# Shorter partition sums, three more low halves on VectorE, an uneven last tile and a new order

## The chip, the cores and the metric

The kernel runs on one core of one Trainium2 chip. A core has a matrix engine (TensorE, PE in the profile; its weight loads are shown as PEld), three engines for elementwise work (VectorE or DVE, ScalarE or ACT, GpSimd or POOL) and SyncE (SP), on whose queue this kernel issues its DMAs. Each engine works through its own stream of instructions in the order in which the kernel recorded them, and waits on semaphores for the others. The metric is the device time in microseconds of one execution, as a median of several.

## The reference

One token mixer with a gate, on x of 2048 tokens by 512 features. With LN for a layer norm without parameters:

```python
xn = LN(x)
# A: attention of 32 heads of 16 features; each token looks at itself and at 7 tokens before it, 2 apart
q, k, v = split(xn @ wqkv)
s = softmax(q . k[t - 0, 2, .., 14] / 4) @ v[t - 0, 2, .., 14] @ wo
# B: an MLP of 1376 hidden features
h = gelu(LN(xn) @ w1 + b1)
g = silu(h @ w2 + b2)
out = x + s * g
```

Tokens that lie before the first are masked in A.

## The kernel before

The host lays x out in two halves (even and odd tokens, `c` = 0 and 1), so that the steps of 2 become steps of 1; each half has 8 tiles of 128 tokens. Numbers in fp32 are fed to TensorE as two fp16 parts: a high part (the rounded number times a power of two) and a low part (the rest); a product is three matmuls, high by high, high by low and low by high. To choose the powers of two, the kernel sums the squares of every weight tensor: ScalarE sums along each partition, and a matmul against a matrix `fours` (128 x 128, every element 4.0) adds over the partitions and gives the sum to all of them (`total`, the matmuls on lines 488 and 493). VectorE then takes the exponent of that sum and makes scales from it.

The work has these parts, by line of the profile:

- Layer norm of the 16 tiles and transposes to features by tokens (`ln0`, lines 690 to 735, for half 0; `ln1`, lines 749 to 765, for half 1).
- 8 attention units (half `c` by group `hb` of 8 heads). TensorE makes q, k and v of a unit (`qkv`, L795 and L802; 96 matmuls of 384 columns for most units); ScalarE, or VectorE for a few, evicts them from PSUM into one of two tiles `U` (L817, L813); DMAs copy shifted rows of k and v (the halo, L825 to L831); VectorE does the attention with products and sums over 2048 numbers per partition (`attention`, L865 and L869 for the logits, L900 to L908 for the softmax, L934, L976 and L929 for the values), helped by GpSimd (L958). The result is split into parts (`emit_o`, L917 and L919) and transposed by DMA (L922) into `oT`.
- The MLP in 44 steps: 4 chunks of 512 tokens by 11 blocks of 128 hidden features. Step p is 12 matmuls into a PSUM tile `mh` (`mlp1`, L1090), GELU on ScalarE (L1107), the high half on ScalarE (L1111) and the low half. The low half has two ways. For the steps in `DVE_LO` VectorE makes it in one instruction (L1115). For the others TensorE subtracts the high half within PSUM, by a matmul against a diagonal matrix `dg` (L1121), and ScalarE reads the rest (L1124). Two steps later 12 matmuls of `mlp2` (L1137) add the block into four PSUM tiles `z`, which ScalarE turns into the gate by SiLU (L1153; L1148 for the last chunk).
- The output projection, 12 matmuls a tile (L1004): for half 0 between the MLP steps, on the two PSUM tiles `ps` that `qkv` uses too (`wo_first`, evicted by VectorE at L1018, added at L995 or on GpSimd at L997); for half 1 at the end (`wo_last`). There the first 9 matmuls of each tile run ahead of the last attention unit's result, the last 3 behind it; VectorE multiplies with the gate (L1069), x is added (L995, L997) and a DMA stores the tile (L998). The last tile is done in two parts of 256 columns, with lines 1060, 1063 and 1065 in place of these.
- `WAKE0 + WAKE` = 34 matmuls of 256 columns against `fours`, read as bf16, whose result nobody uses (L1239): they fill TensorE in the start.

None of this is written in the order of execution. Each operation is given to a planner (`Plan.add`) with an engine, a length, what it reads and writes, and a priority; `issue` orders them all with a list scheduler and records them. With `judge` and `draw` the lengths are varied by a chain of random seeds (`SEEDS`); the chain decides which order comes out. The planner's lengths set the order only.

Of the kernel before, what the change touches and what calls it, by code (L numbers as in the profile page):

```python
# [9 lines left out]
F32 = mybir.dt.float32  # L10
F16 = mybir.dt.float16
BF16 = mybir.dt.bfloat16
# [7 lines left out]
P = 128  # L20
S, D, F = 2048, 512, 1376
# [5 lines left out]
NHB = 4  # L27
# [31 lines left out]

BEFORE_W1 = (0, 1, 4, 5)  # L60

DVE_LO = (*range(4), *range(12, 44))


class Buf:
# [5 lines left out]
    @property  # L71
    def t(self):
        return self.ring.tiles[self.slot]
# [18 lines left out]
class Plan:  # L92
# [245 lines left out]

SEEDS = ((100197, 519502, 511555, 636945, 242082, 583485, 986620, 484517, 932055, 691004, 181636),)

# [45 lines left out]
def tile_mixer(ctx, tc, a_x, a_wqkv, a_wo, b_w1, b_b1, b_w2, out):  # L388
    nc = tc.nc
    pl = Plan()  # L390
# [9 lines left out]
    sb = ctx.enter_context(tc.tile_pool(name="sb", bufs=1))  # L400
# [15 lines left out]
    def dma(nbytes, fn, r, w, **k):  # L416
        pl.add("sp", 0.0, fn, r, w, nbytes=nbytes, **k)

    xv, ov = a_x, out

    PR_H, PR_U, PR_M = 200.0, 1000.0, 1000000.0

    ident = sb.tile([P, P], F32, name="ident")
    make_identity(nc, ident)
    fours = sb.tile([P, P], F32, name="fours")
    nc.vector.memset(fours, 4.0)
    halves = sb.tile([P, 16], F32, name="halves")
    nc.gpsimd.memset(halves[:, 0:8], -0.5)
    nc.gpsimd.memset(halves[:, 8:16], 0.5)
# [11 lines left out]
    oT = sb.tile([P, NHB, 2, 2, 4, P], F16, name="oT")  # L441
# [40 lines left out]

    def total(dst, dkey, cols, n, ckeys, late=False, apart=False):

        b = (R_ps if late else R_z[0]).new()
        if apart:
            for k in range(2):
                pl.add("pe", 0.15, lambda k=k: nc.tensor.matmul(
                    b.t[:, 0:1], fours, cols()[:, k:k + 1], start=(k == 0), stop=(k == 1)),
                    [ckeys[k]], [b], prio=min(pl.prio, PTOT))  # L490
            n = 1
        else:
            pl.add("pe", 0.15, lambda: nc.tensor.matmul(b.t[:, 0:n], fours, cols()[:, 0:n], start=True,
                                                       stop=True), ckeys, [b], prio=min(pl.prio, PTOT))
# [71 lines left out]
    def prep_q(hb):  # L566
# [426 lines left out]
    def finish(c, i, t, tkey, x, eng="dve"):  # L993
        if eng == "dve":
            dve(512, lambda: nc.vector.tensor_tensor(t(), t(), x(), op=ALU.add), tkey, tkey[:1])  # L995
        else:
            pool(1.2, lambda: nc.gpsimd.tensor_tensor(t(), t(), x(), op=ALU.add), tkey, tkey[:1])  # L997
        dma(P * 2048, lambda: nc.sync.dma_start(ov[c, i], t()), tkey[:1], [("out", c, i)], tail=0.7)  # L998

    def wo_mm(b, i, hbs, last=NHB - 1, cols=slice(0, D)):  # L1000
        def mm():
            for hb in hbs:
                for n, (s, t) in enumerate(((0, 0), (0, 1), (1, 0))):
                    nc.tensor.matmul(b.t[:, cols], oT[:, hb, i // 4, s, i % 4], wo[:, t, hb, cols],  # L1004
                                     start=(hb == 0 and n == 0), stop=(hb == last and n == 2))
        return mm
# [19 lines left out]
    def wo_last():  # L1026
        rings = [R_ps, R_ps, R_mh, R_mh] + R_z
        tiles = []

        halfs = [slice(h * 256, h * 256 + 256) for h in range(2)]  # L1030
        for i in range(NI):
            b = rings[i].new()
            bh = [b, rings[0].new()] if i == NI - 1 else [b]
            r = [("oT", hb, i // 4) for hb in range(NHB - 1)] + [("wo", k) for k in (0, 2)]
            if i < NI - 1:
                pe(9, 512, wo_mm(b, i, range(NHB - 1)), r, [b], prio=PR_M * 10 + 2 * i)
            else:

                for h in range(2):
                    pe(9, 256, wo_mm(bh[h], i, range(NHB - 1), cols=halfs[h]), r, [bh[h]], prio=PR_M * 10 + 2 * i + h)  # L1040
            tiles.append(bh)
        for i in range(4):
            dma(P * 2048, lambda i=i: nc.sync.dma_start(gu[i], gd[1, i]),
                [("gd", 1, i), ("U0end",)], [("gu", i)], prio=PR_M * 10)
        for i in range(NI):
            b = tiles[i][0]
            if i < 7:
                xb = R_f.new()
                x, xkey = (lambda xb=xb: xb.t), xb
            else:  # L1050
                x, xkey = (lambda: U[0][:, NI * D:(NI + 1) * D]), ("gux",)
            dma(P * 2048, lambda x=x, i=i: nc.sync.dma_start(x(), xv[1, i]),
                [("oT", NHB - 2, 0), ("U0end",)], [xkey], prio=PR_M * 10 + i)
            t = lambda i=i: gu[i]
            if i == NI - 1:
                for h in range(2):
# [3 lines left out]
                    dve(256, lambda b=b, t=t, cols=cols: nc.vector.scalar_tensor_tensor(  # L1060
                        t()[:, cols], b.t[:, cols], osc[:, 2:3], t()[:, cols], op0=ALU.mult, op1=ALU.mult),
                        [b, ("gu", i), ("osc",)], [("gu", i, h)], port=False, c=0.14)
                    dve(256, lambda t=t, x=x, cols=cols: nc.vector.tensor_tensor(  # L1063
                        t()[:, cols], t()[:, cols], x()[:, cols], op=ALU.add), [("gu", i, h), xkey], [("gu", i, h)])
                    dma(P * 1024, lambda i=i, t=t, cols=cols: nc.sync.dma_start(ov[1, i][:, cols], t()[:, cols]),
                        [("gu", i, h)], [("out", 1, i, h)], tail=0.7)
                continue
            pe(3, 512, wo_mm(b, i, [NHB - 1]), [("oT", NHB - 1, i // 4)], [b], prio=PR_M * 10 + 2 * i + 1)
            dve(512, lambda b=b, t=t: nc.vector.scalar_tensor_tensor(  # L1069
                t(), b.t, osc[:, 2:3], t(), op0=ALU.mult, op1=ALU.mult),  # L1070
                [b, ("gu", i), ("osc",)], [("gu", i)], port=False, c=0.14)
            finish(1, i, t, [("gu", i), xkey], x, "pool" if i % 2 == 0 else "dve")
# [8 lines left out]
    def mlp1(ch, f):  # L1081
# [24 lines left out]
        with prio(PR_H + pl.prio * 1e-6):  # L1106
# [6 lines left out]
                [b] + [("hseq", NF * ch + f - 1)] * (NF * ch + f > 0), [hk, ("hseq", NF * ch + f)])  # L1113
            if NF * ch + f in DVE_LO:
                dve(512, lambda: nc.vector.scalar_tensor_tensor(  # L1115
# [76 lines left out]
    def zero_halo(b):  # L1192
        pool(0.85, lambda: nc.gpsimd.memset(U[b][0:1, KH * P:(KH + 7) * P], 0.0), [],
             [("kz", b)])
# [38 lines left out]
        f()  # L1233
    zero_halo(0)
    zero_halo(1)
    idle = fours.bitcast(BF16)
    for n in range(WAKE0 + WAKE):
        b = R_z[0].new()
        pl.add("pe", 0.2 if n < 16 else 0.1, lambda b=b: nc.tensor.matmul(b.t[:, 0:2 * P], idle[:, 0:P], idle, start=True,  # L1239
                                                       stop=True), [("yd", 2)] if n >= WAKE0 else [], [b], prio=1e9)  # L1240
# [136 lines left out]
    for u, (c, hb) in enumerate(units):  # L1377
# [62 lines left out]
```

## Time and profile before

| | |
|---|---|
| median of 3 runs | 414.87 us (414.87 to 415.22) |
| the profiled execution | 414.88 us, of which the span of the profile is 413.0 |
| TensorE busy | 408.2 us (99%), 2112 matmuls |
| TensorE weight loads | 210.3 us (51%) |
| VectorE busy | 383.7 us (93%), 367 instructions |
| ScalarE busy | 224.2 us (54%) |
| GpSimd busy | 104.2 us (25%) |
| granted clock of TensorE | 1.00 |

A row of a group reads: line, engine, operation, what is written <- what is read, sizes, count | busy us, mean ns of one | idle time of the engine just before, and what ended it. A row of the timeline reads: start, length, engine, line, operation, count, and in brackets the idle time before it with its releaser. In the chain that ended last a row is start, length and what, and each piece starts where the one before it ended. Lengths of matmuls in groups and timelines include the time until the result is out, which lies beside the next matmul; the distance from start to start is what one costs in a stream.

### The profile page before, as it was taken

What the parts mean: (1) busy time and instruction counts of PE and PEld (TensorE: products, weight loads), DVE (VectorE), ACT (ScalarE), POOL (GpSimd) and SP (SyncE); (2) the same over time, 40 slices, a digit from 0 to 9 for tenths busy, and PEclk for the clock granted to TensorE, in tenths of its full rate; (3) what the DMA queues carried; (4) which work ended last, traced back from release to release, by engine and by line L of the source; (5) the groups of instructions that cost most, each with busy time, mean ns of one, the idle gap of its engine ahead of it and who ended that gap; (6) DMA issues with size and microseconds to landing.
All of it is one profiled execution on the core that took longest, in us unless ns stands there. A gap on an engine that the chain in (4) does not pass through costs nothing.

```text
span 413.0 us, 5592 instructions
## 1 busy us (share of the span) xinstructions
PE 408.2 (99%) x2112; PEld 210.3 (51%) x2112; DVE 383.7 (93%) x367; ACT 224.2 (54%) x362; POOL 104.2 (25%) x154
## 2 busy tenths in 40 slices
PE   8999999999999999999999999999999999999996
PEld 5666444445544554456444654445655554444443
DVE  5989999999899999999799979999989999999947
ACT  4999998979469477323663271126411492244500
POOL 7620531003900250015000510055036500250004
PEclk9999999999999999999999999999999999999999
DMA  7972360130253638300650061201053375008025
GB/s 282 414 278 78 110 210 0 63 116 1 71 123 126 143 95 173 61 2 0 150 194 1 2 135 57 102 0 56 22 179 114 102 203 166 2 0 241 16 51 203
DMA packets 42666, 44.83 MB, mean 109 GB/s; under 512 B 27496, under 2 KB 27936, under 8 KB 42128
## 3 DMA queue, kind: packets, MB, share of 16 engines
q1 hardware_dynamic: 42640, 44.49, 35.6%
q8 instruction: 16, 0.26, 0.3%
q14 instruction: 10, 0.08, 0.1%
HBM read 23.53 MB, written 7.34 MB: 75 GB/s over the span
## 4 chain that ended last, share of the span: by engine, by line
PE 97%; DVE 1%; DMA 1%; POOL 0%; issue 0%
PE z L1137 28%; PE ps L795 27%; PE mh L1090 26%; PE ps L1004 6%; PE mh L795 2%; PE z L1004 2%; PE mh L1004 1%; PE ps L1090 1%; PE z L697 1%; PE mh L802 1%; DMA prod<-in_A_x_dram 1%; PE ps L802 1%; PE mh L1121 0%; DVE U L1063 0%; PE z L1239 0%; DVE U L1060 0%
## 5 line engine op out<-in xcount | busy, mean ns | idle before, releaser
L1090 PE MATMUL mh<-yT,w 128*128 128x512 f16 (+1 forms) x504 | 115.5, 379 | 0.0
L795 PE MATMUL ps<-wq,yT 128*128 128x384 f16 x684 | 114.8, 326 | 0.0
L1137 PE MATMUL z<-w,h 128*128 128x512 f16 x480 | 110.7, 379 | 0.0
L795 PEld LDWEIGHTS <-yT 128*128 128x128 f16 x744 | 72.7, 98 | 48.2
L1090 PEld LDWEIGHTS <-w 128*128 128x128 f16 (+1 forms) x528 | 52.9, 100 | 60.8
L1107 ACT ACTIVATE mh<-mh,b1T,hsc 128x512 f32<-128x512 f32 (+1 forms) x42 | 31.4, 748 | 88.5 <-PE mh L1090 88.5
L1137 PEld LDWEIGHTS <-h 128*128 128x128 f16 x480 | 47.0, 98 | 55.6
L865 DVE TENSOR_TENSOR prod<-U 128x2048 f32<-128x2048 f32 x32 | 73.0, 2283 | 1.3 <-DMA U<-U 1.1
L869 DVE TENSOR_REDUCE L<-prod 128x128 f32<-128x2048 f32 x32 | 73.0, 2281 | 0.8
L817 ACT ACTIVATE U<-ps,cs 128x384 f32<-128x384 f32 x57 | 33.0, 579 | 59.9 <-PE ps L795 58.1
L934 DVE TENSOR_TENSOR prod<-L,U 128x2048 f32<-128x2048 f32 x28 | 63.3, 2286 | 0.2
L957 POOL COPY gate<-prod 1x1 f32<-1x1 f32 x21 | 3.6, 174 | 210.6 <-DVE prod L865 210.6
L929 DVE TENSOR_TENSOR prod<-prod,prod 128x2048 f32<-128x2048 f32 x16 | 36.5, 2284 | 0.0
L958 POOL TENSOR_TENSOR prod<-prod 128x1024 f32<-128x1024 f32 x14 | 32.9, 2347 | 0.0
L1004 PEld LDWEIGHTS <-oT 128*128 128x128 f16 x204 | 20.0, 98 | 21.5
L1004 PE MATMUL ps<-wo,oT 128*128 128x512 f16 (+1 forms) x132 | 28.8, 369 | 0.0
L1111 ACT ACTIVATE h<-mh,hsc 128x512 f16<-128x512 f32 x38 | 25.8, 683 | 0.7
L1115 DVE SCALAR_TENSOR_TENSOR h<-mh,hsc,h 128x512 f16<-128x512 f32 x31 | 22.9, 744 | 2.5 <-ACT h L1111 2.3
L958 POOL TENSOR_TENSOR prod<-prod,prod 128x1024 f32<-128x1024 f32 x7 | 16.4, 2346 | 0.0
L997 POOL TENSOR_TENSOR f<-f,f 128x512 f32<-128x512 f32 x4 | 10.6, 2640 | 22.6 <-DVE f L1018 20.6
L997 POOL TENSOR_TENSOR U<-U,f 128x512 f32<-128x512 f32 x4 | 5.9, 1469 | 34.5 <-DVE U L1069 34.5
L919 DVE SCALAR_TENSOR_TENSOR o<-prod,osc,o 128x1024 f16<-128x1024 f32 (+1 forms) x9 | 10.4, 1151 | 3.6 <-ACT o L917 3.6
(182 smaller groups left out, 395.0 us busy)
## 6 DMA issues: line engine op xcount, KB each, us to landing
f<-in_A_x_dram SPq DMA_DIRECT2D x31, 256.0 KB, 3.5
U<-U SPq DMA_DIRECT2D x16, 392.0 KB, 4.0
gd<-f SPq DMA_DIRECT2D x12, 256.0 KB, 2.1
oT<-in_B_w_dram SPq DMA_DIRECT2D x2, 1024.0 KB, 9.4
yT<-in_B_w_dram SPq DMA_DIRECT2D x2, 1024.0 KB
f<-gd SPq DMA_DIRECT2D x8, 256.0 KB, 3.7
out_dram<-f SPq DMA_DIRECT2D x8, 256.0 KB, 3.2
out_dram<-U SPq DMA_DIRECT2D x7, 256.0 KB, 2.0
```

The source lines that it names most:

```text
L795: nc.tensor.matmul(b.t[:, 0:384], y[:, s, k, o:o + P], wq[:, hb, t, k], start=(n == 0), stop=(n == 11))
L817: act(384, lambda i=i, b=b: nc.scalar.activation(U3[:, i:i + 31:15, :], b.t[:, 0:384].rearrange("p (t e) -> p t e", t=3), AF.Identity, sca ...
L865: first = dve(2048, lambda p2=p2, g=g: nc.vector.tensor_tensor(p2(), q, slots(Ut, KH, 2 * g), op=ALU.mult), qk + [("kh", ub, 0), ("kh", ub ...
L869: first.then = dve(2048, lambda pr=pr, g=g: nc.vector.tensor_reduce(L3()[:, 2 * g:2 * g + 2], pr.t.rearrange("p (r f d) -> p r f d", r=2, ...
L929: dve(n, lambda: nc.vector.tensor_tensor(d(), a(), b(), op=ALU.add), keys, [dkey])
L934: dve(2048, lambda: nc.vector.tensor_tensor(pr.t.rearrange("p (r f d) -> p r f d", r=2, d=DH), L3()[:, 2 * g:2 * g + 2].rearrange("p r (f ...
L958: nc.gpsimd.tensor_tensor(x.t[:, 0:1024], x.t[:, 0:1024], y(), op=ALU.add)
L1004: nc.tensor.matmul(b.t[:, cols], oT[:, hb, i // 4, s, i % 4], wo[:, t, hb, cols], start=(hb == 0 and n == 0), stop=(hb == last and n == 2))
L1090: nc.tensor.matmul(b.t[0:M], w1[:, s, k, f * P:f * P + M], yT[ch][:, t, k], start=(n == 0), stop=(n == 11))
L1107: act(512, lambda: nc.scalar.activation(b.t[0:M], b.t[0:M], AF.Gelu_apprx_tanh, bias=b1T[0:M, f:f + 1], scale=hsc[0:M, 1:2]), [b, ("b1T",) ...
L1111: act(512, lambda: nc.scalar.activation(hi()[0:M], b.t[0:M], AF.Identity, scale=hsc[0:M, 2:3]), [b] + [("hseq", NF * ch + f - 1)] * (NF * ...
L1137: nc.tensor.matmul(z.t, hl[s][0:K, t * P:(t + 1) * P], w2[0:K, w, f], start=(f == 0 and n == 0), stop=(f == NF - 1 and n == 2))
```

## The change

Four edits:

- `fours` becomes a bf16 matrix of 128 x 256 elements, each 4.0625. A sum over the partitions reads the upper 16 bits of each fp32 number as bf16 (a view with a step of two), so the matmuls of `total` take bf16 on both sides; 4.0625 in place of 4 makes up for the bits that are cut off. The planner's length for it goes from 0.15 to 0.08.
- `DVE_LO` takes steps 9, 10 and 11 as well. They no longer have L1121 and L1124, but L1115.
- The last tile of `wo_last` is cut into 320 and 192 columns.
- `SEEDS` holds another chain of 14 seeds, and with it the planner gives another order. Most of it is as before; blocks of 12 or 6 matmuls change places, and so do instructions of VectorE and ScalarE and a few DMAs of SyncE's queue. GpSimd's order is the same. ScalarE has 27 table loads where it had 24.

```diff
+LASTC = 320
-DVE_LO = (*range(4), *range(12, 44))
+DVE_LO = (*range(4), *range(9, 44))
...
-SEEDS = ((100197, 519502, 511555, 636945, 242082, 583485, 986620, 484517, 932055, 691004, 181636),)
+SEEDS = ((189, 403599, 34575, 851879, 637112, 551358, 379210, 712317, 150252, 25848, 233642, 161354, 386615,
+          226897),)
...
-    fours = sb.tile([P, P], F32, name="fours")
-    nc.vector.memset(fours, 4.0)
+    fours = sb.tile([P, 2 * P], BF16, name="fours")
+    nc.vector.memset(fours, 4.0625)
...
     def total(dst, dkey, cols, n, ckeys, late=False, apart=False):
+        upper = lambda a, n: cols()[:, a:a + n].bitcast(BF16)[:, 1:2 * n:2]
         b = (R_ps if late else R_z[0]).new()
         if apart:
             for k in range(2):
-                pl.add("pe", 0.15, lambda k=k: nc.tensor.matmul(
-                    b.t[:, 0:1], fours, cols()[:, k:k + 1], start=(k == 0), stop=(k == 1)),
+                pl.add("pe", 0.08, lambda k=k: nc.tensor.matmul(
+                    b.t[:, 0:1], fours[:, 0:P], upper(k, 1), start=(k == 0), stop=(k == 1)),
...
-            pl.add("pe", 0.15, lambda: nc.tensor.matmul(b.t[:, 0:n], fours, cols()[:, 0:n], start=True,
+            pl.add("pe", 0.08, lambda: nc.tensor.matmul(b.t[:, 0:n], fours[:, 0:P], upper(0, n), start=True,
...
-        halfs = [slice(h * 256, h * 256 + 256) for h in range(2)]
+        halfs = [slice(0, LASTC), slice(LASTC, D)]
...
-                for h in range(2):
-                    b, cols = tiles[i][h], halfs[h]
-                    pe(3, 256, wo_mm(b, i, [NHB - 1], cols=cols), [("oT", NHB - 1, i // 4)], [b],
+                for h, cols in enumerate(halfs):
+                    b, m = tiles[i][h], cols.stop - cols.start
+                    pe(3, m, wo_mm(b, i, [NHB - 1], cols=cols), [("oT", NHB - 1, i // 4)], [b],
...
-    idle = fours.bitcast(BF16)
+    idle = fours
```

More of the change, by code (lines that the diff above doesn't have):

```diff
@@ L1037, in wo_last @@
             else:
-                for h in range(2):
-                    pe(9, 256, wo_mm(bh[h], i, range(NHB - 1), cols=halfs[h]), r, [bh[h]], prio=PR_M * 10 + 2 * i + h)
+                for h, cols in enumerate(halfs):
+                    pe(9, cols.stop - cols.start, wo_mm(bh[h], i, range(NHB - 1), cols=cols), r, [bh[h]], prio=PR_M * 10 + 2 * i + h)
             tiles.append(bh)
@@ L1055, in wo_last @@
             if i == NI - 1:
-                for h in range(2):
-                    b, cols = tiles[i][h], halfs[h]
-                    pe(3, 256, wo_mm(b, i, [NHB - 1], cols=cols), [("oT", NHB - 1, i // 4)], [b],
+                for h, cols in enumerate(halfs):
+                    b, m = tiles[i][h], cols.stop - cols.start
+                    pe(3, m, wo_mm(b, i, [NHB - 1], cols=cols), [("oT", NHB - 1, i // 4)], [b],
                        prio=PR_M * 10 + 2 * i + h - 0.5)
-                    dve(256, lambda b=b, t=t, cols=cols: nc.vector.scalar_tensor_tensor(
+                    dve(m, lambda b=b, t=t, cols=cols: nc.vector.scalar_tensor_tensor(
                         t()[:, cols], b.t[:, cols], osc[:, 2:3], t()[:, cols], op0=ALU.mult, op1=ALU.mult),
                         [b, ("gu", i), ("osc",)], [("gu", i, h)], port=False, c=0.14)
-                    dve(256, lambda t=t, x=x, cols=cols: nc.vector.tensor_tensor(
+                    dve(m, lambda t=t, x=x, cols=cols: nc.vector.tensor_tensor(
                         t()[:, cols], t()[:, cols], x()[:, cols], op=ALU.add), [("gu", i, h), xkey], [("gu", i, h)])
-                    dma(P * 1024, lambda i=i, t=t, cols=cols: nc.sync.dma_start(ov[1, i][:, cols], t()[:, cols]),
+                    dma(P * 4 * m, lambda i=i, t=t, cols=cols: nc.sync.dma_start(ov[1, i][:, cols], t()[:, cols]),
                         [("gu", i, h)], [("out", 1, i, h)], tail=0.7)
```

## The prediction

> **What bounds the kernel now.** I read the page first, then the chain that ended last piece by piece, then the waits of VectorE and ScalarE, and last the timeline of the places that the change touches.
>
> ```profile
> span 413.0 us, 5592 instructions
> PE 408.2 (99%) x2112; PEld 210.3 (51%) x2112; DVE 383.7 (93%) x367; ACT 224.2 (54%) x362; POOL 104.2 (25%) x154
> PE 97%; DVE 1%; DMA 1%; POOL 0%; issue 0%
> ```
>
> TensorE holds 97% of the chain; VectorE, at 93%, is the only other engine near the bound. So two questions decide: how much TensorE work leaves, and whether VectorE, which gets more, stays ahead of TensorE. The rows of the chain that the change touches (start, length, what):
>
> ```profile
> 6.08 0.11 PE z L1239
> 22.38 0.12 PE z L493 x2
> 92.27 0.22 PE mh L1121
> 95.08 5.85 PE ps L795 x36
> 100.93 0.22 PE mh L1121
> 121.26 0.22 PE mh L1121
> 402.81 5.21 PE z L1004 x30
> 408.02 0.02 issue
> 409.93 0.42 DVE U L1063
> ```
>
> Each piece starts where the one before it ended; from 13 us to 408 us no wait of TensorE stands in the chain. The row of 402.81 has 18 matmuls of 512 and 12 of 256 columns, by columns 24 of 512: 5.21/24 = 0.216 us each; the row of 95.08 gives 5.85/36 = 0.1625 us for 384 columns. Every instruction taken out of TensorE's stream is therefore worth its full length, as long as nothing else comes late. The sum below goes against the profiled execution's own 414.88 us, 0.01 above the median of 414.87; 0.2% (0.83 us) is about what tells a time from no change.
>
> **Three low halves to VectorE.** Steps 9, 10 and 11 of the 44 MLP steps lose their matmul at L1121, which are the three chain rows at 92.27, 100.93 and 121.26: 3 x 0.216 = 0.65 us off the path. The work moves here:
>
> ```profile
> L1115 DVE SCALAR_TENSOR_TENSOR h<-mh,hsc,h 128x512 f16<-128x512 f32 x31 | 22.9, 744 | 2.5 <-ACT h L1111 2.3
> L1124 ACT ACTIVATE h<-mh,hsc 128x512 f16<-128x512 f32 x7 | 4.8, 683 | 3.1 <-PE mh L1121 3.1
> L1107 ACT ACT_TABLE_LOAD x10 | 12.8, 1283 | 0.2
> ACT mh L1107 <- PE mh L1090: 88.5, 32, 8.9
> ```
>
> VectorE gets 3 x 0.744 = 2.2 us. ScalarE loses 3 x 0.683 = 2.0 us, but the new order has three table loads more (3 x 1.283 = 3.8 us): 1.8 us net. ScalarE waits 88.5 us for MLP matmuls alone, so that is hidden. VectorE's 2.2 us need cover, and these are its idle times that end with something TensorE paces:
>
> ```profile
> 113.52 2.29 DVE L865 TENSOR_TENSOR prod<-U 128x2048 f32<-128x2048 f32 x1 [1.08 <-DMA U<-U]
> 165.58 0.75 DVE L1115 SCALAR_TENSOR_TENSOR h<-mh,hsc,h 128x512 f16<-128x512 f32 x1 [1.13 <-ACT h L1111]
> 199.03 1.28 DVE L919 SCALAR_TENSOR_TENSOR o<-prod,osc,o 128x1024 f16<-128x1024 f32 x1 [1.58 <-ACT o L917]
> 241.19 1.28 DVE L919 SCALAR_TENSOR_TENSOR o<-prod,osc,o 128x1024 f16<-128x1024 f32 x1 [1.21 <-ACT o L917]
> 304.41 0.75 DVE L1018 SCALAR_TENSOR_TENSOR f<-ps,osc,f 128x512 f32<-128x512 f32 x1 [1.27 <-issue]
> ```
>
> Two of the three low halves stand ahead of 113.5: 1.4 us late against 1.08 idle. The third makes it 1.0 late, and 1.13 idle at 165.6 takes that up; 1.58, 1.21 and 1.27 follow. I cost the move at nothing on VectorE. If that cover is gone, the first to wait is TensorE's reuse of PSUM in the first output projection (rival B).
>
> At the end the cover is wide:
>
> ```profile
> 395.16 0.75 DVE L919 SCALAR_TENSOR_TENSOR o<-prod,osc,o 128x512 f16<-128x512 f32 x1 [0.79 <-ACT o L917]
> oT<-o SPq DMA_TRANSPOSE x2, 3.0
> ```
>
> The last transpose lands near 395.9 + 3.0 = 398.9, and TensorE wants it at 402.81, the last pass over tiles 4 to 7: 3.9 us, of which 1.2 go because TensorE comes earlier.
>
> **Sums over the partitions.** Nine matmuls against `fours` turn from fp32, which the trace shows as two passes, into one bf16 pass. Two are in the start; seven (L493) stand in the steady stream:
>
> ```profile
> 22.22 0.28 PE L493 MATMUL z<-s,fours 128*128 128x2 f32 x2
> 22.36 0.32 PE L795 MATMUL mh<-wq,yT 128*128 128x384 f16 x1
> ```
>
> The sum holds the stream for 22.36 - 22.22 = 0.14 us. The trace has no single bf16 pass of so few columns. Its bounds: it could vanish (0.14 saved each), or the next weight load could stay exposed (0.03 saved each, worked out under rival A). I take half of the pair, 0.07 saved, as one of two passes goes: 7 x 0.07 = 0.49 us, between 0.2 and 1.0. The two in the start I cost at nothing: the new order puts one more of the filling matmuls of L1239 (0.11, the row at 6.08) ahead of the first three transposes and one more near 13 us, which eats about what the sums give back there, 2 x 0.07 and some 0.1 us of waiting; plus or minus 0.1 us.
>
> **The last tile in 320 and 192 columns.** The tail by timeline:
>
> ```profile
> 407.84 1.47 PE L1004 MATMUL ps<-wo,oT 128*128 128x256 f16 x12
> 409.15 0.27 PE L1239 MATMUL z<-fours 128*128 128x256 bf16 x1
> 408.04 0.48 DVE L1060 SCALAR_TENSOR_TENSOR U<-z,osc,U 128x256 f32<-128x256 f32 x1 [0.17 <-PE z L1004]
> 408.56 0.94 DVE L1063 TENSOR_TENSOR U<-U 128x256 f32<-128x256 f32 x1
> 409.42 0.47 DVE L1060 SCALAR_TENSOR_TENSOR U<-ps,osc,U 128x256 f32<-128x256 f32 x1
> 407.13 0.74 DVE L1069 SCALAR_TENSOR_TENSOR U<-z,osc,U 128x512 f32<-128x512 f32 x1
> 407.94 1.27 POOL L997 TENSOR_TENSOR U<-U,f 128x512 f32<-128x512 f32 x1 [1.29 <-DVE U L1069]
> ```
>
> Twelve matmuls of 256 columns take 409.15 - 407.84 = 1.31 us, 0.109 each; 64 columns more or less are a quarter of that, 0.027. The first part ends 12 x 0.027 = 0.32 us later, the second takes 0.32 less: TensorE ends where it did. On VectorE 64 columns are (0.74 - 0.48)/4 = 0.065 us. Counted on the clock of before: L1060 of 320 columns 408.36 to 408.9, then L1063 at 0.42 + 0.07 = 0.49 (the row of 0.42), to 409.4; the 0.94 of the first L1063 lay beside GpSimd's L997, and the new order lets L1069 of tile 6 pass the add of tile 5, so that L997 starts some 0.7 us earlier and is done. The second part follows at 409.42 as before and ends 2 x 0.065 = 0.13 earlier. The moved add of tile 5 can push the pair back by some 0.05, so I take 0.10 us off. Ends: 0.2 off, and 0.2 on if the short matmuls are held by their weights (rival A).
>
> **The redrawn order.** The same blocks change places on TensorE: 12 L1137 matmuls go ahead of the second group of 96 L795, 6 each ahead of the next three; the first output projection starts two MLP blocks later; one pass of L1004 moves behind the last MLP step. Permuted work costs TensorE nothing unless a producer is late. On SyncE's queue the load of `wo` goes ahead of one load of an x tile, and the later transposes and halo copies trade places with stores. I looked at three tight places. (1) The second group of 96 starts some 1.6 us later than now (12 x 0.216 less 1.0 saved), so unit 3's halo copies do too; VectorE, about 1 us late there, idles some 0.5 us, which the 1.13 at 165.6 covers. (2) A second sum for `wo` waits for ScalarE:
>
> ```profile
> 87.17 1.04 ACT L480 ACTIVATE wo<-yT 128x1024 bf16<-128x1024 f32 x1
> 89.17 0.28 PE L493 MATMUL ps<-s,fours 128*128 128x2 f32 x2
> ```
>
> The new order puts one L1124 (0.68) ahead of that L480: 88.2 + 0.7 = 88.9, against 89.17 less the 0.3 that four sums ahead of it have saved. No margin is left there; what it can lose is in rival C. (3) PSUM in the first output projection, under B. I cost the order at 0, from -0.1 to the losses of the rivals.
>
> **Sum.** 0.65 + 0.49 + 0.10 = 1.24 us off 414.88: 413.6 us.
>
> **Rival A, weights hold the small matmuls.**
>
> ```profile
> L1004 PEld LDWEIGHTS <-oT 128*128 128x128 f16 x204 | 20.0, 98 | 21.5
> ```
>
> A load of 128 columns lasts 0.098 us, and no pair of load and matmul in the steady stream is spaced under the 0.109 of the tail. If about that is a floor, a bf16 sum costs 0.109 and saves 0.03 (7 x 0.03 = 0.22), and 12 matmuls of 192 columns take 12 x 0.109 in place of 12 x 0.082: 0.32 later, a net loss of 0.2 in the tail. Then 0.65 + 0.22 - 0.2 = 0.67 off: 414.2 us, within 0.2%. For it speaks the length of the load; against it that the 0.109 of 256 columns is half the 0.216 of 512, so there the columns set the pace and not the load. I give it 0.18. The Trainium skill speaks to it on both sides. "TensorE: Matmul & The Clock Gate", section LDWEIGHTS, gives a load as its columns over 1.2, an estimate of 107 ns for 128, which would hold the 192 columns; its section Back-to-back issue gap gives some 81 ns for a sustained pair at 128 columns, which would not, and would leave the sums 0.06 each. The trace's 98 ns lies between and shows no pair short enough to decide.
>
> **Rival B, VectorE comes late (slower).** Its place is the first output projection, where L795 and L1004 share two PSUM tiles:
>
> ```profile
> 307.28 0.74 DVE L1018 SCALAR_TENSOR_TENSOR f<-ps,osc,f 128x512 f32<-128x512 f32 x1
> 306.74 4.06 PE L795 MATMUL ps<-wq,yT 128*128 128x384 f16 x24
> ```
>
> The second dozen of L795 starts at 306.74 + 12 x 0.1625 = 308.69, on the tile that an L1018 before it freed at 308.02: 0.67 us of margin, behind the 1.27 idle at 304.41. VectorE may be 1.9 us late there; beyond that each us is lost whole, since TensorE runs to the end. Slower than before by 0.83 needs 1.24 + 0.83 more: 4.0 us late. With nothing absorbed it would be 2.2 us from the low halves, 1.6 from the halo copies of unit 3 and 0.6, half a table load, from an Exp behind one: 4.4 late, 2.5 lost, 416.1 us. Against it speak the five waits above, each of which would have to vanish. Chance 0.15.
>
> **Rival C, it does not do what it says.** The matmuls leave, but TensorE gets waits in the new order: at place (2), and at the L1121 that remain, each behind a ScalarE whose instructions have changed places. Two such waits of 0.3 us: 414.2 us. Chance 0.12.
>
> **How the numbers follow.** The forecast of 413.6 has 0.55, with its own range of 413.0 to 414.0 from the bounds of the sums and the tail. A and C lie at 414.2, within 0.2%, but their faster edge is past it: 0.05 of them counts as faster. So 0.60 faster, 0.24 same, 0.16 slower. The range takes in forecast, A, C and the mild part of B: 413.0 to 415.1.
>
> **What would show it.** L1121 with 5 rows and L1115 with 39; no wait of TensorE in the chain after 14 us; the spacing from each bf16 sum to the next matmul, 0.07 or 0.11; the spacing of the 192-column matmuls, 0.08 or 0.11; L1018 in the first output projection still waiting for TensorE. The prediction is wrong if the chain holds VectorE or ScalarE pieces between 14 and 407 us, or if the start up to 14 us is longer by over 0.3 us.

## The result and the profile after

The changed kernel takes 413.5 us (median of 6 runs, 413.24 to 414.17), against 415.1 for the kernel before on the same chip (6 runs, 414.87 to 415.53). The ratio is 0.9964, with a 95% interval of 0.9952 to 0.9976: faster by 0.24 to 0.48%. The forecast was 413.6. Ratios further down are to the kernel before too, run beside each kernel on the same chip.

The profiled execution of the changed kernel is the slowest of its six: 414.17 us, span 412.3. Its page has, against the lines shown of before:

```profile
span 412.3 us, 5567 instructions
PE 407.2 (99%) x2100; PEld 208.3 (51%) x2100; DVE 385.8 (94%) x370; ACT 226.8 (55%) x362; POOL 104.3 (25%) x154
PE 97%; DMA 1%; DVE 1%; SPq 0%; POOL 0%; issue 0%
```

TensorE still holds 97% of the chain. VectorE has 2.1 us more work. The chain, row by row (start, length, what):

```profile
1.64 5.24 DMA prod<-in_A_x_dram
...
14.57 0.65 PE ps L801 x4
...
23.14 0.00 PE z L499
...
86.18 0.21 PE mh L1127
...
402.14 5.53 PE z L1010 x30
...
407.69 0.56 DVE U L1066
...
408.28 0.64 DVE U L1069
408.92 0.34 DVE U L1066
...
409.28 0.36 DVE U L1069
```

```profile
L1127 PE MATMUL mh<-h,dg 128*128 128x512 f16 x5 | 1.9, 379 | 0.0
L1121 DVE SCALAR_TENSOR_TENSOR h<-mh,hsc,h 128x512 f16<-128x512 f32 x33 | 24.3, 740 | 1.5 <-ACT h L1117 1.3
```

The second fence has groups of instructions. In this kernel's numbering the lines around the change stand 6 higher: L1127 is the matmul against `dg` that was L1121, L1121 the low half on VectorE that was L1115, L801 was L795, L1096 was L1090, L1143 was L1137, L1010 was L1004. Five matmuls against `dg` are left; the 33 low halves on VectorE are those of the commonest shape, and 6 of two other shapes make 39. Between 14 and 407 us the chain holds no piece of another engine, and the sums (L499) have almost no length in it.

I split the span at two rows of the chain: the first `ps` row of four matmuls, which ends the start, and the first matmul of the last pass over tiles 4 to 7, which begins the tail. Before, these stand at 13.81 and 402.81 us.

```profile
13.81 0.65 PE ps L795 x4
```

| us | before | after | difference |
|---|---|---|---|
| start | 13.81 | 14.57 | +0.76 |
| steady stretch | 389.00 | 387.57 | -1.43 |
| last pass to the end of VectorE's last instruction | 7.54 | 7.50 | -0.04 |

The span is 0.7 us shorter in this execution. The start took 0.76 away from a gain of some 1.5, and the question is whose that start is. The first x tile landed as before: VectorE begins with it at 3.52 us, before at 3.50. The second x tile, issued 0.9 us after the first, is the load of 5.24 us with which the chain begins here, and VectorE waits for it. Before, the chain began with the first tile's load (2.75 us), and VectorE came to the second tile without a wait. VectorE's row for the second tile, before and in the changed kernel:

```profile
6.00 0.68 DVE L654 BATCH_NORM_STATS2 bn<-prod 128x6 f32<-128x512 f32 x1
```

```profile
6.91 0.69 DVE L660 BATCH_NORM_STATS2 bn<-prod 128x6 f32<-128x512 f32 x1 [0.80 <-DMA prod<-in_A_x_dram]
```

A kernel below with the same order up to the tail (the last tile in 256 and 256 columns) didn't wait for that tile, and its first row of four stands 0.08 earlier than before:

```profile
5.94 0.69 DVE L660 BATCH_NORM_STATS2 bn<-prod 128x6 f32<-128x512 f32 x1
```

```profile
13.73 0.65 PE ps L801 x4
```

Over all the kernels profiled here, one execution of each, the row of four lies between 13.73 and 14.66 us. In the changed order it stands at 13.73 to 13.90 in four kernels, at 14.33 to 14.66 in the five whose chain begins with the late load, and at 14.03 and 14.44 in two that don't wait for that tile. And a kernel below that has the order before and the same instructions up to there has it at 14.19, 0.38 later than before. So the start differs from one execution to the next, and the 0.76 of this one can't be put down to the change. Whether the changed order starts late more often is not shown, nor that the start makes most of the spread of 0.9 us between runs of one kernel, though that is likely. The steady stretch is the measure used below, with the times beside it: it is 387.57 us in each of the three kernels that should have it alike. In some of the expectations quoted below it is 387.74 and 389.17, since I had taken its start from the timeline (14.40), where the last pass was taken from the chain (402.14); from the chain alone it is 387.57 and 389.00, and the differences are the same.

### The profile page after: what moved, and what is told of

It reads as the page before. It is cut to its first block, busy times and chain, and to the rows that moved or that the text cites. A ratio compares the mean times of both kernels' runs of the same rounds, so it can differ in the third digit from the quotient of the medians.

```text
span 412.3 us, 5567 instructions
## 1 busy us (share of the span) xinstructions
PE 407.2 (99%) x2100; PEld 208.3 (51%) x2100; DVE 385.8 (94%) x370; ACT 226.8 (55%) x362; POOL 104.3 (25%) x154
## 4 chain that ended last, share of the span: by engine, by line
PE 97%; DMA 1%; DVE 1%; SPq 0%; POOL 0%; issue 0%
PE z L1143 28%; PE ps L801 27%; PE mh L1096 26%; PE ps L1010 6%; PE mh L801 2%; PE z L1010 2%; DMA prod<-in_A_x_dram 1%; PE mh L1010 1%; PE ps L1096 1%; PE z L703 1%; PE mh L808 1%; PE mh L1127 0%; DVE U L1069 0%; PE z L1245 0%; DVE U L1066 0%; PE ps L808 0%
## 5 line engine op out<-in xcount | busy, mean ns | idle before, releaser
L1096 PE MATMUL mh<-yT,w 128*128 128x512 f16 (+1 forms) x504 | 115.5, 379 | 0.0
L801 PE MATMUL ps<-wq,yT 128*128 128x384 f16 x684 | 114.3, 326 | 0.0
L1143 PE MATMUL z<-w,h 128*128 128x512 f16 x480 | 110.7, 379 | 0.0
L801 PEld LDWEIGHTS <-yT 128*128 128x128 f16 x744 | 72.4, 98 | 48.4
L1096 PEld LDWEIGHTS <-w 128*128 128x128 f16 (+1 forms) x528 | 52.9, 100 | 60.9
L1113 ACT ACTIVATE mh<-mh,b1T,hsc 128x512 f32<-128x512 f32 (+1 forms) x42 | 31.4, 749 | 82.7 <-PE mh L1096 81.7
L1143 PEld LDWEIGHTS <-h 128*128 128x128 f16 x480 | 46.7, 98 | 55.8
L823 ACT ACTIVATE U<-ps,cs 128x384 f32<-128x384 f32 x57 | 32.9, 580 | 62.5 <-PE ps L801 60.6
L1010 PEld LDWEIGHTS <-oT 128*128 128x128 f16 x204 | 19.8, 98 | 21.8
L1010 PE MATMUL ps<-wo,oT 128*128 128x512 f16 (+1 forms) x132 | 28.4, 367 | 0.0
L1121 DVE SCALAR_TENSOR_TENSOR h<-mh,hsc,h 128x512 f16<-128x512 f32 x33 | 24.3, 740 | 1.5 <-ACT h L1117 1.3
L1003 POOL TENSOR_TENSOR f<-f,f 128x512 f32<-128x512 f32 x4 | 10.6, 2641 | 20.6 <-DVE f L1024 18.7
L923 ACT ACTIVATE o<-prod,osc 128x1024 f16<-128x1024 f32 (+1 forms) x9 | 9.4, 1045 | 9.3 <-DVE prod L935 6.2
L1003 POOL TENSOR_TENSOR U<-U,f 128x512 f32<-128x512 f32 x4 | 5.9, 1470 | 33.1 <-DVE U L1075 33.1
```

What stands on the lines that cost most here:

```text
L801: nc.tensor.matmul(b.t[:, 0:384], y[:, s, k, o:o + P], wq[:, hb, t, k], start=(n == 0), stop=(n == 11))
L823: act(384, lambda i=i, b=b: nc.scalar.activation(U3[:, i:i + 31:15, :], b.t[:, 0:384].rearrange("p (t e) -> p t e", t=3), AF.Identity, sca ...
L1096: nc.tensor.matmul(b.t[0:M], w1[:, s, k, f * P:f * P + M], yT[ch][:, t, k], start=(n == 0), stop=(n == 11))
L1113: act(512, lambda: nc.scalar.activation(b.t[0:M], b.t[0:M], AF.Gelu_apprx_tanh, bias=b1T[0:M, f:f + 1], scale=hsc[0:M, 1:2]), [b, ("b1T",) ...
L1143: nc.tensor.matmul(z.t, hl[s][0:K, t * P:(t + 1) * P], w2[0:K, w, f], start=(f == 0 and n == 0), stop=(f == NF - 1 and n == 2))
```

## The experiments

Each kernel keeps the written order of one of the two kernels (the planner sees the same operations and lengths) and changes only what its operations do. So an effect isn't mixed with another order.

**Sums in fp32 again.**

```diff
-    fours = sb.tile([P, 2 * P], BF16, name="fours")
-    nc.vector.memset(fours, 4.0625)
+    fours = sb.tile([P, P], F32, name="fours")
+    nc.vector.memset(fours, 4.0)
...
-            pl.add("pe", 0.08, lambda: nc.tensor.matmul(b.t[:, 0:n], fours[:, 0:P], upper(0, n), start=True,
+            pl.add("pe", 0.08, lambda: nc.tensor.matmul(b.t[:, 0:n], fours, cols()[:, 0:n], start=True,
...
```

> The changed kernel with its order and everything else kept, but the sums over the partitions in fp32 again. Measured on the steady stretch, from the first of the four-matmul groups of L801 (14.40 us in the changed kernel's trace) to the first matmul of the last pass over tiles 4 to 7 (402.14): 387.74 us in the changed kernel, 389.17 before. My reading of the trace of after (a bf16 sum holds the stream for 0.028 us, an fp32 one for 0.14): 7 x 0.112 = 0.78 longer, 388.52, and the time 0.8 to 1.0 us above the changed kernel. By the price in my forecast (0.07 each) 388.23. If weights held a bf16 sum to 0.109 (rival A) 387.96. If it is the order and not the sums that the stretch was shortened by, 387.74.

Measured: steady stretch 388.35, 0.78 longer than in the changed kernel; 414.53 us, ratio to before 0.9986 (0.9977 to 0.9995). The sums are worth 0.78 us, not the 0.49 of the forecast. The timeline of the changed kernel, and then of this one, shows one of them:

```profile
22.98 0.17 PE L499 MATMUL z<-s,fours 128*128 128x2 bf16 x1
23.00 0.32 PE L801 MATMUL mh<-wq,yT 128*128 128x384 f16 x1
```

```profile
22.93 0.28 PE L499 MATMUL z<-s,fours 128*128 128x2 f32 x2
23.07 1.14 PE L801 MATMUL mh<-wq,yT 128*128 128x384 f16 x6
```

From start to start a bf16 sum holds the stream for 0.028 us (to three decimals 22.977 to 23.005), two fp32 passes for 0.14: seven times 0.112 is 0.78.

**Nine sums for each.** Is the short matmul cheap only as a single one, since the load of its weights hides beside a long matmul?

```diff
-            pl.add("pe", 0.08, lambda: nc.tensor.matmul(b.t[:, 0:n], fours[:, 0:P], upper(0, n), start=True,
-                                                       stop=True), ckeys, [b], prio=min(pl.prio, PTOT))
+            pl.add("pe", 0.08, lambda: [nc.tensor.matmul(b.t[:, 0:n], fours[:, 0:P], upper(0, n), start=True,
+                                                        stop=True) for _ in range(9)], ckeys, [b], prio=min(pl.prio, PTOT))
```

> The changed kernel with each of the seven sums of the steady stream done nine times in a row into the same place (56 bf16 matmuls of 1 to 5 columns more, each with its own load of 128 columns of weights). If one always holds the stream for 0.028 us: steady stretch 387.74 + 56 x 0.028 = 389.3. If a single short matmul is cheap only since the loads around it hide beside long matmuls, and a row of them is paced by its loads (0.098 by their recorded length): 387.74 + 56 x 0.098 = 393.2. That would leave the reason of rival A standing, and only its use here wrong.

Measured: 388.97, 1.40 longer for 56 matmuls more, 0.025 us each; 414.77 us in one run. One row of nine in the timeline, and what follows:

```profile
22.20 0.37 PE L499 MATMUL z<-s,fours 128*128 128x2 bf16 x9
22.43 0.97 PE L801 MATMUL mh<-wq,yT 128*128 128x384 f16 x5
```

Nine pairs of load and matmul pass in 0.23 us, though each load is recorded with 0.096. So here the recorded length of a load is how long it takes and not how often one can start; the loads overlap. Rival A falls with its reason, not only in its use. These nine load the same matrix each time; the next kernels have short matmuls that load parts of `oT`.

**The last tile in 256 and 256, and in 384 and 128 columns.** The plan keeps the lengths for 320 and 192; the edit of the first kernel is shown, the second has 384 in place of 256.

```diff
-LASTC = 320
+LASTC, PLANC = 256, (320, 192)
...
-                    b, m = tiles[i][h], cols.stop - cols.start
+                    b, m = tiles[i][h], PLANC[h]
```

> The changed kernel with its order kept, but the last tile in two parts of 256 columns. Measured from the first matmul of the last pass over tiles 4 to 7 to the end of the span: 10.16 us in the changed kernel, 10.19 before. My forecast: 0.10 longer with 256, 10.26. What the trace of after suggests, where VectorE's add of the first part still lies beside GpSimd's L1003: 0.0 to 0.05 longer. Rival A, weights hold 192 columns: 0.2 shorter, 9.96. Time: not to be told from the changed kernel, 413.5.

> The changed kernel with its order kept, but the last tile in 384 and 128 columns. If columns alone set the pace: 128-column matmuls 0.055 us apart, TensorE ends where it did. If loads of weights pace them: 0.098 apart, TensorE ends 12 x 0.043 = 0.5 later. VectorE's first part ends later by 0.13, the second part has 0.13 less: the end of VectorE follows its own queue behind the first part, so the tail from the last pass on is 10.16, plus or minus 0.1, in the first case, and 10.3 to 10.6 in the second.

Measured: steady stretch 387.57 in both, as in the changed kernel. From the last pass to the end of VectorE's last instruction 7.56 us with 256, 7.50 with 320, 7.67 with 384; to the end of the span, as the expectations count, 10.21, 10.14 and 10.18. Times: 413.42 us (ratio 0.9967, 0.9955 to 0.998) and 413.66 in one run, not to be told from the changed kernel. The tail of the changed kernel by timeline, and the short matmuls of the kernel with 128:

```profile
406.91 1.65 POOL L1003 TENSOR_TENSOR U<-U,f 128x512 f32<-128x512 f32 x1
407.49 1.15 PE L1010 MATMUL ps<-wo,oT 128*128 128x192 f16 x12
407.69 0.55 DVE L1066 SCALAR_TENSOR_TENSOR U<-z,osc,U 128x320 f32<-128x320 f32 x1 [0.26 <-PE z L1010]
408.28 0.64 DVE L1069 TENSOR_TENSOR U<-U 128x320 f32<-128x320 f32 x1
408.48 0.27 PE L1245 MATMUL z<-fours 128*128 128x256 bf16 x1
```

```profile
407.27 0.83 PE L1010 MATMUL ps<-wo,oT 128*128 128x128 f16 x12
407.94 0.27 PE L1245 MATMUL z<-fours 128*128 128x256 bf16 x1
```

Twelve matmuls of 192 columns take 408.48 - 407.49 = 0.99 us, 0.083 each, and of 128 columns 0.67, 0.056 each: at these widths columns alone set the pace. The tail gains 0.04 of the 0.10 forecast, and 0.06 against 256 and 256 columns in the same order. GpSimd's last L1003, which was the L997 at 407.94, starts earlier, but counted from the last pass only by 0.36 us (4.77 in place of 5.13), and it takes 1.65 in place of 1.27. It ends where it did, 6.42 us behind the start of that pass in place of 6.40, so VectorE's L1069 of the first part still lies beside it: 0.64 us in place of 0.49. VectorE's last pair starts at 408.84, 0.36 behind TensorE's last matmul, as soon as VectorE's own queue is free; before it was 0.27 behind, and waited for VectorE too.

**The three low halves back on TensorE, and the order alone.** In the first kernel steps 9, 10 and 11 get their matmul and ScalarE's read where the plan has VectorE's instruction. The second has, beside this, fp32 sums and 256 and 256 columns, so that only the order is left of the change.

```diff
-                dve(512, lambda: nc.vector.scalar_tensor_tensor(
+                dve(512, lambda: (nc.tensor.matmul(b.t[0:M], dg[0:M, 0:M], hi()[0:M], start=False, stop=True, skip_group_check=True),
+                                  nc.scalar.activation(lo()[0:M], b.t[0:M], AF.Identity, scale=hsc[0:M, 2:3])) if NF * ch + f in (9, 10, 11) else nc.vector.scalar_tensor_tensor(
...
```

> The changed kernel with its order kept, but the low halves of steps 9, 10 and 11 made by TensorE and ScalarE again. If the three matmuls are worth their length, as forecast: steady stretch 387.74 + 0.65 = 388.39 us, time 414.1, and VectorE's busy time 2.2 less with no effect. If VectorE's 2.2 us had cost something (a mild rival B), less than 0.65 is lost; if TensorE waits for ScalarE at the matmuls that come back, more than 0.65, and the chain shows ScalarE.

> The order of the changed kernel with all three other edits taken back: fp32 sums, 256 and 256 columns, the three low halves on TensorE. If the order costs nothing, as forecast: steady stretch 389.17 us, time as before, 414.9 to 415.1. If the order itself saved something, 388.2 to 388.9 and a time below 414.6; if it costs, above 389.5. The start, up to the first L801, shows whether the 0.76 us that the changed kernel's profiled execution was later at 14 us belongs to the order (then it is here too) or to the landing of the first x tile (5.24 us there, 2.75 before) in that one execution.

Measured: steady stretch 389.86 and 390.65, 2.29 and 3.08 longer than in the changed kernel; times 415.85 (ratio 1.0022, 1.0013 to 1.003) and 416.98 (1.0048, 1.0035 to 1.006). The two differ by 0.79, which is the sums again. Only 0.65 of the 2.29 is the matmuls; the rest is waiting. ScalarE's timeline of the first kernel at the place of the longest wait, and TensorE's row behind it:

```profile
100.62 0.68 ACT L1122 ACTIVATE hlast<-mh,hsc 96x512 f16<-96x512 f32 x1 [1.23 <-PE mh L1121]
101.21 0.57 ACT L823 ACTIVATE U<-ps,cs 128x384 f32<-128x384 f32 x1
```

```profile
101.82 9.91 PE L801 MATMUL ps<-wq,yT 128*128 128x384 f16 x60 [1.24 <-ACT U L823]
```

The low half of step 10 (L1122) stands in ScalarE's queue ahead of an eviction (L823) that frees a PSUM tile of q, k and v. It waits for its own matmul (L1121 at 100.20), which stands in TensorE's stream behind 36 matmuls of `qkv`; so the eviction comes late, and TensorE waits for the tile. By starts TensorE loses 1.40 us here, and 0.24 at step 9, whose low half stands ahead of the split of `wo` (L541): 1.64, which is the 2.29 less the 0.65. This order fits work on VectorE and not on ScalarE. Since the place of the matmul comes from a plan that has none, this doesn't price the low halves alone. The next two kernels ask from the other side.

The second kernel also answers for the start. Its row of four stands late, at 14.65, with a load of 5.32 us for the second x tile, and in the first kernel, with the same order, it stands at 13.78; so it is the load and not the order. The 5.24 and 2.75 in the expectation are the loads of two different x tiles, the second and the first.

**The order before, with the edits.** First only the three low halves move, in the order of before; then all edits but the order are made. VectorE's instruction stands where ScalarE's stood.

```diff
-            pe(1, 512, lambda: nc.tensor.matmul(b.t[0:M], dg[0:M, 0:M], hi()[0:M], start=False,
-                                                stop=True, skip_group_check=True),
+            pe(1, 512, lambda: NF * ch + f in (9, 10, 11) or nc.tensor.matmul(
+                b.t[0:M], dg[0:M, 0:M], hi()[0:M], start=False, stop=True, skip_group_check=True),
...
-            act(512, lambda: nc.scalar.activation(lo()[0:M], b.t[0:M], AF.Identity,
-                                                  scale=hsc[0:M, 2:3]), [b], [h])
+            act(512, lambda: nc.vector.scalar_tensor_tensor(lo()[0:M], b.t[0:M], hsc[0:M, 2:3], hi()[0:M], op0=ALU.mult, op1=ALU.subtract) if NF * ch + f in (9, 10, 11)
+                else nc.scalar.activation(lo()[0:M], b.t[0:M], AF.Identity, scale=hsc[0:M, 2:3]), [b], [h])
```

> The kernel before with its order kept, but the low halves of steps 9, 10 and 11 on VectorE, where ScalarE's L1124 stood in the plan. By rows of the chain alone the steady stretch (first ps row of four matmuls to the last pass over tiles 4 to 7) is 389.00 us before and 387.57 in the changed kernel. Forecast: 3 x 0.216 off, 388.35, and a time of 414.4. Rival, from the run with four low halves each (TensorE's L1096 waited 4.0 us for PSUM that L1121 reads): with an order that was not drawn for it, a low half waits behind a product of 2.2 us in VectorE's queue, and TensorE's reuse of that PSUM tile waits with it: the gain is eaten, 389.0 or more, and the chain shows VectorE ahead of an L1090.

> All edits of the change but the order: the order before, with bf16 sums, the last tile in 320 and 192 columns and the three low halves on VectorE. If the order is worth nothing (forecast): steady stretch 387.57 us as in the changed kernel, time 413.5. If the redrawn order is what lets the low halves pass unseen: 387.57 plus what the run with the low halves alone loses, 388.2 to 389.5, with waits of TensorE for VectorE or ScalarE between 90 and 170 us.

Measured: 388.93 and 388.57, against 389.00 before and 387.57 in the changed kernel. Times: 415.12 (ratio 0.9999, 0.9991 to 1.0008) and 414.74 (0.9994, 0.9985 to 1.0003). The low halves alone bring 0.07 us in place of 0.65, and without the redrawn order 1.00 us of the whole gain is missing. The place is the same in both; first VectorE's and TensorE's timeline of the kernel with the low halves alone (it has before's numbering, and the low half of step 11 is L1124), then those of the changed kernel:

```profile
121.22 2.28 DVE L934 TENSOR_TENSOR prod<-L,U 128x2048 f32<-128x2048 f32 x1
123.42 0.74 DVE L1124 SCALAR_TENSOR_TENSOR h<-mh,hsc,h 128x512 f16<-128x512 f32 x1
...
121.04 2.75 PE L1137 MATMUL z<-w,hlast 97*128 97x512 f16 x12
124.22 2.75 PE L1090 MATMUL mh<-yT,w 128*128 128x512 f16 x12 [0.42 <-DVE h L1124]
```

```profile
118.98 0.65 DVE L1121 SCALAR_TENSOR_TENSOR h<-mh,hsc,h 128x512 f16<-128x512 f32 x1
119.55 0.68 DVE L914 TENSOR_TENSOR L<-L,mx 128x512 f32<-128x512 f32 x1
120.14 0.16 DVE L655 TENSOR_TENSOR cT<-lw 128x8 f32<-128x8 f32 x1
120.26 4.49 DVE L940 TENSOR_TENSOR prod<-L,U 128x2048 f32<-128x2048 f32 x2
...
123.23 2.75 PE L1096 MATMUL mh<-yT,w 128*128 128x512 f16 x12
```

A low half reads the PSUM tile `mh`, and there are two of them. The 12 matmuls two steps later can't start before it is read. In the old order it stands behind a product of 2.28 us and ends at 124.16. TensorE's 12 L1137 from 121.04 on take 12 x 0.216 = 2.59, so the next L1090 could start at 123.63; it starts at 124.22, 0.59 lost of the 0.65 gained. (The bracket's 0.42 counts from the end of the last matmul's result and not from where the next could start, and so is 0.16 short.) With all edits TensorE is earlier and loses 1.00 there, again 0.16 more than the bracket:

```profile
124.09 2.75 PE L1096 MATMUL mh<-yT,w 128*128 128x512 f16 x12 [0.84 <-DVE h L1130]
```

In the new order the low half stands ahead of the product, ends at 119.63, and is wanted at 123.23.

**More work for VectorE.** How much can it still take? Steps 9 to 11 make their low half four times, then twice.

```diff
-                dve(512, lambda: nc.vector.scalar_tensor_tensor(
+                dve(512, lambda: [nc.vector.scalar_tensor_tensor(
                     lo()[0:M], b.t[0:M], hsc[0:M, 2:3], hi()[0:M], op0=ALU.mult,
-                    op1=ALU.subtract), [b, hk], [h], port=False, c=0.14)
+                    op1=ALU.subtract) for _ in range(4 if NF * ch + f in (9, 10, 11) else 1)], [b, hk], [h], port=False, c=0.14)
```

> The changed kernel with the low halves of steps 9, 10 and 11 made four times each by VectorE: nine instructions of 0.744 us, 6.7 us of VectorE more, from 113 to 155 us. Forecast's view: VectorE's idles behind them (0.87, 0.51, 1.21, 0.97, 0.62 us in the trace of after, 4.2 in all) and the slack at the first output projection take it up, TensorE loses under 0.5 us; VectorE's share rises by 6.7 us of busy time. Rival B's mechanism with a hard edge: 6.7 less 4.2 of cover is 2.5 late, all lost: 416.0, with TensorE waiting for VectorE at L801 or L1010 behind L1024 near 300 us.

> The changed kernel with the low halves of steps 9, 10 and 11 made twice each: 2.2 us of VectorE more. With four each (6.7 us more) the steady stretch grew by 5.21 us, so some 1.5 us were covered. If that cover is a fixed amount: 2.2 - 1.5 = 0.7 longer, 388.3 us. If the loss goes in proportion: 5.21 x 2.2 / 6.7 = 1.7 longer, 389.3. Forecast's view, five idles of VectorE take it up: 387.57.

Measured: 392.78 and 388.09, 5.21 and 0.52 longer than the changed kernel; times 419.18 (ratio 1.0092, 1.0077 to 1.0108) and 414.34 (0.9981, 0.9972 to 0.999). The waits of TensorE with four, then the place with two (its VectorE row and its TensorE row), then the same rows of the changed kernel behind the one idle time ahead of them:

```profile
PE mh L1096 <- DVE h L1121: 4.0, 3, 1.9
PE ps L801 <- ACT U L823: 0.5, 1, 0.5
```

```profile
133.07 0.75 DVE L1121 SCALAR_TENSOR_TENSOR h<-mh,hsc,h 128x512 f16<-128x512 f32 x1
...
133.87 2.75 PE L1096 MATMUL mh<-yT,w 128*128 128x512 f16 x12 [0.35 <-DVE h L1121]
```

```profile
114.52 2.29 DVE L871 TENSOR_TENSOR prod<-U 128x2048 f32<-128x2048 f32 x1 [0.87 <-DMA U<-U]
...
131.92 0.75 DVE L1121 SCALAR_TENSOR_TENSOR h<-mh,hsc,h 128x512 f16<-128x512 f32 x1
...
133.59 2.75 PE L1096 MATMUL mh<-yT,w 128*128 128x512 f16 x12
```

With four both expectations miss: more is lost than either has, and not at the first output projection. TensorE waits for low halves near 125 to 139 us, and once, at 99 us, for an eviction on ScalarE (the place is the same as with five more low halves, below). The cover is a fixed amount. In the changed kernel the low half at 131.92 ends at 132.67, and TensorE starts 0.92 later, of which 0.05 is the way from one to the other (133.82 to 133.87 with two). 0.87 here and 0.87 idle at 114.5 are 1.74 us, and the low halves that are repeated (at 92.71, 98.01 and 118.98 in the changed kernel) all stand ahead of this place. From start to start a repeated low half holds VectorE for 0.78 us, so two each cost 2.34 and four each 7.04. Less the 0.52 and 5.21 that were lost, 1.82 and 1.83 us were covered: the same both times, and within 0.1 of the 1.74.

**More low halves on VectorE.** The same edit as in the order before, in the changed kernel, for steps 4 to 8 (the five that are left), and then for 7 and 8 alone.

> The changed kernel with its order kept, but the five low halves of steps 4 to 8 that were left to TensorE made by VectorE too. If VectorE has cover: 5 x 0.216 = 1.08 us off, 412.4, steady stretch 386.66. If its 5 x 0.744 = 3.7 us come late for the evictions of q, k and v or the splits of weights between 75 and 115 us: TensorE waits, and 413.5 or more.

> The changed kernel with its order kept, and the low halves of steps 7 and 8 on VectorE as well. All five of steps 4 to 8 brought 1.13 us of loss: 1.08 gained, 2.2 lost where ScalarE's first eviction L823 stood behind L541, which waits for the scale of wo from VectorE (L518). In the changed kernel that eviction has some 1.3 us to spare. Two cost 1.5 us of VectorE, of which up to 0.8 was taken up there, and bring TensorE 0.43 earlier: between 387.14 us (no wait, 0.43 gained) and 387.73 (0.6 late). Below 387.57 it beats the changed kernel.

Measured: 388.70 for five, 1.13 longer than the changed kernel and 414.49 us (ratio 0.9989, 0.998 to 0.9998); 387.16 for two, 0.41 shorter, and 413.30 us (0.9958, 0.9944 to 0.9971). With two the two matmuls' 0.43 comes out nearly whole. With five TensorE waits in the waits view, and ScalarE's timeline shows for what; the last row is that of the changed kernel:

```profile
PE ps L801 <- ACT U L823: 1.7, 1, 1.7
PE mh L1096 <- DVE h L1130: 0.2, 1, 0.2
```

```profile
96.21 1.15 ACT L541 ACTIVATE wo<-yT,osc 128x1024 f16<-128x1024 f32 x1 [4.18 <-DVE osc L518]
```

```profile
93.55 1.15 ACT L541 ACTIVATE wo<-yT,osc 128x1024 f16<-128x1024 f32 x1 [0.76 <-DVE osc L518]
```

ScalarE's L541 waits for VectorE's scale for `wo` (L518) and starts 2.66 us later, with the evictions of q, k and v queued behind, so TensorE waits for the PSUM tile. With two, no wait of TensorE is left in the view, and the steady stretch is the shortest of all. By time that kernel beats the kernel before, but can't be told from the changed one: the two intervals overlap for the most part.

## Why the prediction was right, and where it was not

The time of 413.6 is 0.1 from the measured median, and that near it is partly luck. The trace's own sum is 1.43 + 0.04 us off before the start is counted, beside 1.24 forecast, and the kernel before, from whose 414.88 I took them off, has a median of 415.1 over the six runs: a base that was too low made up for a gain that was too small. Some terms are wrong in their reasons, too. By its steps:

- **What bounds the kernel.** Right. TensorE holds the chain from 14 to 407 us, and what leaves its stream comes out at full length where no producer comes late.
- **Three low halves, 0.65.** Right in size for the changed kernel: 1.43 less the 0.78 of the sums is 0.65. The reason I gave for their cover was wrong. I costed VectorE's 2.2 us "at nothing" from five idle times, and named PSUM in the first output projection as the first thing to wait. The five idles don't lie where a delay is due. With 2.2 us more, the first thing to wait is a matmul of the MLP (L1090, now L1096) for the PSUM tile that a late low half reads, and there the changed kernel has 0.87 us to spare. Four of the five idles I counted on lie behind that place.
- **The redrawn order, 0.** It is worth 1.00 us in this change. The step was argued from the old kernel's producers; I weighed three tight places of the order and none of the low halves' own places in VectorE's queue. In the old order step 11's low half would have stood behind a product of 2.28 us. I had the gain of the low halves and the price of the order in two terms that only hold together.
- **Seven sums, 0.49.** The mechanism was right, the size was not: 0.78. I took half of the fp32 pair; a bf16 pass is a fifth of it (0.028 of 0.14), less than either spacing, 0.07 or 0.11, that I had named as a sign. The bounds of 0.2 and 1.0 held it.
- **The tail, 0.10.** It gave 0.04. The step that failed is "L997 starts some 0.7 us earlier and is done": counted from the last pass it starts 0.36 earlier, takes longer and ends where it did, and the add of the first part lay beside it.
- **The start, 0 ± 0.1.** 13.73 to 13.90 us in the four kernels of the new order that have the early start, against 13.81 before: within 0.1. The profiled execution's 0.76 later is the late landing of the second x tile, so the sign that I had named for a wrong prediction (the start longer by over 0.3) speaks of one execution and not of the change.
- **The redrawn order's table loads.** Hidden, as forecast: ScalarE idles 82.7 us ahead of its GELUs in the changed kernel.
- **Rival A** is refuted by the 0.025 of a sum and the 0.056 of 128 columns. **Rival B** didn't come, and its place isn't where VectorE binds first; its mechanism, a late VectorE holding a PSUM tile, is the one that the runs with more work for VectorE show, some 170 us earlier. **Rival C** didn't come in the changed kernel. Its mechanism, TensorE behind a ScalarE that is late, is what the low halves cost when they are put back on TensorE in the new order.
- **The chances.** The rivals' terms add up to 0.25 and 0.15, where I wrote 0.24 same and 0.16 slower.

The Trainium skill's page "TensorE: Matmul & The Clock Gate", section Back-to-back issue gap, gives the isolated gap as the columns over 2.4 plus 2.5 ns, and in its table a floor of some 25 ns up to 64 columns. This case agrees with that in a stream of loads and matmuls: 0.025 us for the repeated sums, 0.056 for 128 columns, 0.083 for 192. Its other figure, 81 ns for a sustained pair at 128 columns, and its section LDWEIGHTS, read as a price per pair, are not borne out here.

The three tight places of the order: none of them shows in the chain of the changed kernel, which has no wait of TensorE there.

## What to carry to other kernels

When work moves to an engine that is nearly full, don't add up its idle time: look, for each instruction that moves, at what stands ahead of it in its new queue, which buffer it holds, and when the bound engine wants that buffer again. An edit and an order that was drawn for it belong in one term; each alone can be worth nothing. And a short matmul between long ones cost 0.028 us here, not the 0.096 that its weight load is recorded with.

## What the hardware showed that I had not expected

- Pairs of a weight load (128 columns, recorded with 0.096 us) and a bf16 matmul of 1 to 5 columns follow each other every 0.025 us, nine in a row.
- Two fp32 passes of 2 columns take 0.14 us where one bf16 pass takes 0.028: five times as long, not twice.
- The landing of one of the first loads moves the whole execution: with the second x tile 5.24 us under way, VectorE waits 0.80 us for it, and the steady stretch begins 0.84 us later than in a kernel with the same instructions up to there whose tile was there in time.
